# A planned HGRN2 + ReGLU kernel: new waits for the first loads and weight slices, one score mask on ScalarE and GpSimd, and even FFN groups

## The chip, the core and the metric

The kernel runs on one core of a Trainium2 chip. The metric is the device time of one execution in microseconds (us). TensorE is called PE here, VectorE DVE, ScalarE ACT, GpSimd POOL and SyncE SP, as the profile has them.

## What is computed

A gated linear attention is followed by a gated feed-forward layer. For 4 batches and 8 heads of 48 columns, 768 tokens each:

```python
f = 1.0 / (1.0 + np.exp(-f_logit))
for t in range(S):
    state = f[:, :, t, :, None] * state + einsum('bhd,bhe->bhde', k[:, :, t], v[:, :, t])
    y[:, :, t] = einsum('bhd,bhde->bhe', q[:, :, t], state)
x = y.transpose(0, 2, 1, 3).reshape(3072, 384)
out = (np.maximum(x @ w_gate, 0) * (x @ w_val)) @ w_out      # 384 -> 1536 -> 384
```

Inputs and output are float32; the kernel works in bfloat16 on PE.

## The kernel before

**Tiling.** The attention is done in chunks. Six *units* take 256 tokens of one batch each (`attention_unit(d, b)`; units 0 to 3 are d = 0 with b = 0 to 3, units 4 and 5 are d = 1 with b = 0, 1). The rest is done in chunks of 128 tokens (`attention_front` and `attention`). For a unit, f, k, q and v are loaded (one DMA of 384 KB each, named f0, k0, ... by unit). ACT takes the log of the gate (exp, then ln: L615, L617). PE sums it along the tokens (L626, L627), and ACT exponentiates the sums (L639, L642). POOL scales k (L644) and DVE scales q (L647) into `hats`. PE transposes these (L678), and DVE and ACT copy them to SBUF (L686, L687). PE makes the scores (L722) in four PSUM banks. DVE multiplies each bank with a causal mask (`seen`, L727) into `ptm`. POOL spreads v into `vpad` (L653). PE makes the states (L699), the products of masked scores and v (`intra`, L757, in two halves for units 0 and 1), and the product with the state (`inter`, L740). The result is copied to `xT` (L781 on ACT, L782 on DVE), the input of the FFN.

**FFN.** `ffn_hidden` makes a gate and a value product of three matmuls each (L959) for one of 12 columns j of 128. ACT takes the relu (L965), and DVE multiplies both (L970) into `gT`. `ffn_out` (L996) multiplies with w_out. A pair of units gives 512 tokens. `groups` says which j are done for each half of the tokens alone (256 columns) and which for all (512 columns). For the first pair `lead = 3` puts three gates ahead of their values.

**Weights.** w_gate and w_val come in three slices each (wg0, wv0 hold j = 0 to 2; wg1, wv1 hold 3 to 5; wg2, wv2 hold 6 to 11) and w_out in three (wo0 to wo2). POOL issues these DMAs (L534), and they convert to bfloat16. SP issues all other DMAs: loads of units (L500) and of chunks (L512), transposes by DMA from unit 4 on (L577, L583), and stores (L1016).

**Order.** The program is made once, ahead of the run. Every operation is recorded with its engine, reads, writes and an assumed duration. `Plan` then lists the operations of each engine in the order in which a model of the chip would start them. `Rings` is its model of DMA. Each engine runs its list in order, and an instruction waits on semaphores for what it reads. So an assumed duration changes only the order; no work depends on it. The list `first` orders the first loads and weight slices by hand: `f2` is a load that waits for nothing and `f3@wg1` is one whose issue waits until the slice wg1 has landed. Since SP and POOL are in order, all that stands behind such a wait is held too. Loads that follow wait for an earlier one, so that `flight` = 3 (units) or 4 (chunks) are under way. Gaps that the model leaves on PE before 24 us are filled with idle matmuls (L1077), which keep PE busy and yield nothing.

```python
first = "f0 k0 wg0@k0 q0 f1 v0 wv0@v0 wg1 wv1@k0+wg0 wg2@f0+wv0 wv2@wg1 q1 k1 wo1@k1+wv1 v1 f2
         wo0@f2+wg2 wo2@f1+wv2 f3@wg1 q2@wg0 k2 v2@wv2 q3@wg0 v3@wg0 k3"
groups = {0: [(0, 2, range(0, 6)), (2, 4, range(0, 6)), (0, 4, range(6, NJ))],
          1: [(0, 2, range(0, 4)), (2, 4, range(0, 4)), (0, 4, range(4, NJ))],
          2: [(0, 2, range(0, 3)), (2, 4, range(0, 3)), (0, 4, range(3, NJ))]}
```

Of the kernel before, what the change touches and what calls it, by code (L numbers as in the profile page):

```python
# [45 lines left out]
class Rings:  # L46
# [19 lines left out]

    def through(self, t, work, n, mine=None):

        for a, b, left in self.other[n]:
            if b <= t:  # L70
                continue
            if t < a:
                if work <= a - t:
                    return t + work
                work -= a - t
                t = a
            left = left if mine is None else mine
            if work <= (b - t) * left:
                return t + work / left
            work -= (b - t) * left  # L80
            t = b
        return t + work

    def room(self):
        over = self.pushed - self.AHEAD
# [12 lines left out]

    def hw(self, op, at, took):
        begin = max(at + (took - 0.05 if op.ring == "turn" else op.lat), self.hw_free)  # L100
        if op.descs == 1024 and self.log:
            self.skew = 0.65 * min(1.0, max(0.0, 1.0 - (self.hw_free - at - took) / 1.2))
        else:
            self.skew = 0.0
        self.hw_free = self.through(begin, op.flow, 1)
        self.made[0].append((begin, self.hw_free, 1.0))
        self.log.append((begin, self.hw_free, self.pushed, op.descs))
        self.pushed += op.descs
        late = 0.0 if at < 5.0 or op.descs < 500 else self.LATE[2 if op.ring == "turn" else at > self.EARLY]
        return self.hw_free + late + (0.8 if op.ring == "turn" else self.LAND + self.skew)  # L110

    def sw(self, at, flow):
        work, left, tail, rest, lag = flow
        begin = max(at, self.sw_free)
        main = self.through(begin, work, 0, 1.0 - left)
        self.sw_free = main + tail
        self.made[1].append((begin, main, left))
        self.made[1].append((main, self.sw_free, rest))
        return self.sw_free + self.LAND + lag


class Plan:
# [209 lines left out]
def bass_hgrn2_outer__then__ffn_reglu_kernel(  # L332
# [95 lines left out]

    def fill(eng, name, ap, value, cols, prio, key=None):
        e = engine[eng]  # L430
        add(eng, lambda: e.memset(ap, value), [], [key or name], occ=0.06 + cols / 1000.0, prio=prio)

    def triangle(t, name, base, prio, step=-1):
        fill("POOL", name, t[:], 1.0, 128, prio)
        add("POOL", lambda: gp.affine_select(out=t[:], in_=t[:], compare_op=ALU.is_ge, fill=0.0, base=base,
                                             pattern=[[1, 128]], channel_multiplier=step),
            [name], [name], occ=0.3, prio=prio)

    for t, name, base in ((upto, "upto", 0), (below, "below", -1)):
        triangle(t, name, base, -20)  # L440
# [1 line left out]
    fill("POOL", "ident", ident[:], 0.0, 128, -16)  # L442
    add("POOL", lambda: gp.affine_select(out=ident[:], in_=ident[:], compare_op=ALU.not_equal, fill=1.0,
                                         base=0, pattern=[[-1, 128]], channel_multiplier=1),
        ["ident"], ["ident"], occ=0.3, prio=-16)
    for i in range(2):
        for t, name, base in ((seen[i], f"seen{i}", -i), (later[i], f"later{i}", 64 - i)):
            fill("POOL", name, t[:], 1.0, 128, -15)
            add("POOL", lambda t=t, base=base, i=i: gp.affine_select(out=t[:], in_=t[:], compare_op=ALU.is_ge, fill=0.0, base=base,
                                                                     pattern=[[i, 2], [1, 64]], channel_multiplier=-1),  # L450
                [name], [name], occ=0.3, prio=-15)
# [41 lines left out]
    def load_unit(n, d, b, after=()):  # L493
        t = ld[n]
        row = NL[n] * 2 * HD
        c, pr = 2 * d + b // 2, b % 2
        src = bass.AP(tensor=srcs[n].tensor, offset=b * H * S * D + 2 * d * C * D, ap=[[2 * D, 128], [S * D, H], [1, 2 * D]])
        dst = bass.AP(tensor=t, offset=slot_of(n, c, pr) * 2 * HD, ap=[[row, 128], [2 * D, H], [1, 2 * D]])
        last = tails.get("load")
        op = add("SP", lambda: sy.dma_start(dst, src), [], in_keys(n, c, 2 * pr, 2 * pr + 2), occ=0.5, lat=1.13,  # L500
                 prio=d * 200 + b * 10, after=after, follows=[last] if last else [])
        tails["load"] = op
        dma(op, f"{n}{slot_of(n, c, pr)}" , 1.79 if n == "f" and d + b == 0 else 1.24 if d == 0 else 1.45, 1, 1024)
        return op

    def load(n, c, b0, b1, after=()):
# [18 lines left out]
    def load_w(nm, s, after):  # L525
        j0, j1 = WB[nm][s:s + 2]
        if nm == "wo":
            src = bass.AP(tensor=w_out.tensor, offset=j0 * 128 * DM, ap=[[DM, 128], [128 * DM, j1 - j0], [1, DM]])
            dst = wo[:, j0:j1, :]
        else:  # L530
            src = bass.AP(tensor=wsrc[nm].tensor, offset=j0 * 128, ap=[[DFF, 128], [128 * DFF, NK], [1, (j1 - j0) * 128]])
            dst = (wg if nm == "wg" else wv)[:, :, j0 * 128:j1 * 128]
        last = tails.get("load_w")
        op = add("POOL", lambda: gp.dma_start(dst, src), [], [f"{nm}{s}"], occ=0.8, lat=2.05, prio=0 if nm != "wo" and s < 1 else 20, after=after,  # L534
                 follows=[last] if last else [])
        tails["load_w"] = op
        dma(op, f"{nm}{s}", (2.0, 0.22, 0.7, 0.5, 0.0) if nm == "wo" else (1.47, 0.25, 0.7, 0.85, 0.9 if s < 1 else 0.2) if j1 - j0 < 6 else (2.9, 0.14, 0.3, 0.3, 0.0), ring="sw")
        return op

    loads, done = [], {}  # L540
# [59 lines left out]
    def attention_unit(d, b):  # L600
# [113 lines left out]
        for i in range(2):  # L714
# [9 lines left out]
                return mm  # L724
            chain("scores", "PE", scores, [k_ for k_ in both if k_[-2] == "0" or k_.startswith(f"qkT{q0 + i}_")], sj, occ=0.215, lat=PE_L, prio=P + 5, opens=sj, tile="64x64")
            for j in range(2):
                add("DVE", lambda i=i, j=j, s=sj[j]: ve.tensor_tensor(  # L727
                    ptm_all[:, m0 + i, j, :, :], s.ap[:, :].rearrange("p (n t) -> p n t", n=NP),
                    seen[i][:].rearrange("p i t -> p (i t)").unsqueeze(1).to_broadcast([128, NP, C]), ALU.mult),
                    [sj[j], f"seen{i}"], [f"ptm{m0 + i}_{j}"], prio=P + 6, **dve_t(512))  # L730
                pk.append(f"ptm{m0 + i}_{j}")
        if d:
            states()
# [210 lines left out]

    hidden = [0]

    def ffn_hidden(c, b0, b1, j, queue=None):
# [8 lines left out]
        def proj(bank, wt):  # L956
# [10 lines left out]
        def values():  # L967
            chain("ffn", "PE", proj(val, wv), xk + [w_key("wv", j)], [val], occ=pe_t(n, n, n), lat=PE_L,
                  prio=P + 1000, opens=[val])
            add("DVE", lambda: ve.tensor_tensor(gT[gi][:, j, n0:n1], relu[ri][:, 0:n], val.ap[:, 0:n], ALU.mult),  # L970
                [val, f"relu{ri}"], [f"gT{gi}_{j}_{b}" for b in range(b0, b1)], prio=P, **dve_t(n))

        if queue is None:
            values()
        else:
            queue.append(values)

    OJ = 4
    held = {}
# [6 lines left out]
    def ffn_out(g, bs, cuts=(0, DM)):  # L986
# [16 lines left out]
        for b, z in [(b, z) for b in bs for z in parts]:  # L1003
# [16 lines left out]
            if z == (0, DM):  # L1020
                tails[f"osb{oi}"] = op

    groups = {0: [(0, 2, range(0, 6)), (2, 4, range(0, 6)), (0, 4, range(6, NJ))],
              1: [(0, 2, range(0, 4)), (2, 4, range(0, 4)), (0, 4, range(4, NJ))],
              2: [(0, 2, range(0, 3)), (2, 4, range(0, 3)), (0, 4, range(3, NJ))]}
    pend = []
    for c in range(NC):
        if c in units:
# [15 lines left out]
                    attention(c, b + e)  # L1044
        for b0, b1, js in groups.get(c, [(0, 4, range(NJ))]):
            len0, js = len(pend), list(js)
            lead = 3 if c == 0 and b1 == 2 else 0
            queue = []
            for j in js[:lead]:
                ffn_hidden(c, b0, b1, j, queue)  # L1050
            for values in queue:
                values()
# [25 lines left out]

    fillers, at, begun = {}, pl.free0["PE"], False
    for op in order["PE"]:  # L1080
        gap, (n, each, rest) = op.start - at, (66, 0.055, 0.25) if at < 5.0 else (128, 0.107, 0.3)
# [82 lines left out]
```

## Time and profile before

| what | value |
|---|---|
| median of 3 runs | 193.06 us (192.57 to 194.32) |
| the profiled execution, its own time | 193.54 us |
| its span (first to last instruction) | 191.8 us |
| PE busy | 184.1 us (96%) |
| DVE, ACT, POOL busy | 106.6, 107.9, 71.7 us |
| read from HBM | 25.95 MB |
| first useful matmul, first FFN matmul | 5.72 us, 15.61 us |
| first FFN matmul of 512 columns (slice wg2) | 30.70 us |

PE's busy time includes the idle matmuls and the time in which its clock is halved, so the 96% are not all useful work. The row of slices in the profile shows the granted clock as PEclk in tenths. A chain of waits is read from its end: each piece was released by the one ahead of it.

### The profile page before, as it was taken

What the parts mean: (1) busy time and instruction counts of PE and PEld (TensorE: products, weight loads), DVE (VectorE), ACT (ScalarE), POOL (GpSimd) and SP (SyncE); (2) the same over time, 40 slices, a digit from 0 to 9 for tenths busy, and PEclk for the clock granted to TensorE, in tenths of its full rate; (3) what the DMA queues carried; (4) which work ended last, traced back from release to release, by engine and by line L of the source; (5) the groups of instructions that cost most, each with busy time, mean ns of one, the idle gap of its engine ahead of it and who ended that gap; (6) DMA issues with size and microseconds to landing.
All of it is one profiled execution on the core that took longest, in us unless ns stands there. A gap on an engine that the chain in (4) does not pass through costs nothing.

```text
span 191.8 us, 5282 instructions
## 1 busy us (share of the span) xinstructions
PE 184.1 (96%) x2209; PEld 111.3 (58%) x2209; DVE 106.6 (56%) x202; ACT 107.9 (56%) x236; POOL 71.7 (37%) x112
## 2 busy tenths in 40 slices
PE   8878699999999999999999999999999999999995
PEld 8747476466686556766445565654555555554554
DVE  5277744739996879453477284643624723443300
ACT  3865478625399765655937739548442543334322
POOL 8667521066375193863552735700900000000000
PEclk9999979999999999999999999999999999999999
DMA  5999999989998999999989989777852120011113
GB/s 152 318 251 219 218 244 205 230 234 285 235 254 157 175 225 171 233 237 231 214 173 194 196 171 223 166 156 172 178 121 71 44 82 8 33 41 44 41 48 116
DMA packets 102343, 32.45 MB, mean 169 GB/s; under 512 B 95408, under 2 KB 102320, under 8 KB 102320
## 3 DMA queue, kind: packets, MB, share of 16 engines
q1 hardware_dynamic: 98336, 28.58, 68.2%
q0 software_dynamic: 3984, 3.54, 11.4%
q8 instruction: 17, 0.28, 0.6%
q14 instruction: 6, 0.05, 0.1%
HBM read 25.95 MB, written 4.72 MB: 160 GB/s over the span
## 4 chain that ended last, share of the span: by engine, by line
PE 85%; DMA 7%; SPq 4%; DVE 3%; POOL 0%; issue 0%; ACT 0%
PE ps L959 49%; PE ps L996 23%; DMA v_in<-in_v_dram 7%; SPq L500 4%; PE ps L757 2%; PE ps L872 2%; DVE ptm L727 1%; PE ps L805 1%; PE ps L902 1%; PE ps L740 1%; PE ps L699 1%; DVE hats L647 1%; PE ps L722 1%; PE ps L912 1%; PE ps L935 1%; PE ps L908 1%
## 5 line engine op out<-in xcount | busy, mean ns | idle before, releaser
L970 DVE TENSOR_TENSOR gT<-relu,ps 128x512 bf16<-128x512 bf16 (+1 forms) x85 | 50.8, 603 | 55.2 <-PE ps L959 39.3
L959 PE MATMUL ps<-xT,wg 128*128 128x512 bf16 (+1 forms) x255 | 61.1, 350 | 0.5 <-ACT xT L781 0.5
L959 PE MATMUL ps<-xT,wv 128*128 128x512 bf16 (+1 forms) x255 | 60.9, 348 | 0.0
L965 ACT ACTIVATE relu<-ps 128x512 bf16<-128x512 f32 (+1 forms) x85 | 44.8, 533 | 28.3 <-PE ps L959 28.2
L996 PE MATMUL ps<-wo,gT 128*128 128x384 bf16 (+2 forms) x312 | 52.0, 314 | 0.0
L996 PEld LDWEIGHTS ps<-wo,gT 128*128 128x128 bf16 x312 | 28.2, 98 | 18.1
L959 PEld LDWEIGHTS ps<-xT,wg 128*128 128x128 bf16 x255 | 24.3, 99 | 20.4 <-ACT xT L781 0.7
L959 PEld LDWEIGHTS ps<-xT,wv 128*128 128x128 bf16 x255 | 24.0, 98 | 19.7
L1011 ACT ACTIVATE osb<-ps 128x384 f32<-128x384 f32 (+2 forms) x25 | 11.7, 474 | 30.6 <-PE ps L996 30.5
L827 POOL TENSOR_TENSOR hats<-k_in,expo 128x384 bf16<-128x384 f32 x12 | 11.8, 996 | 23.2 <-ACT expo L815 12.1
L879 DVE TENSOR_TENSOR ptm<-ps,tri 128x512 bf16<-128x512 f32 x24 | 15.2, 684 | 4.1 <-PE ps L872 4.1
L644 POOL TENSOR_TENSOR hats<-k_in,expo 128x384 bf16<-128x384 f32 x12 | 12.6, 1064 | 11.0 <-DMA k_in<-in_k_dram 8.1
L727 DVE TENSOR_TENSOR ptm<-ps,seen 128x512 bf16<-128x512 f32 x24 | 14.9, 681 | 1.3 <-PE ps L722 1.2
L830 POOL TENSOR_TENSOR hats<-q_in,expo 128x384 bf16<-128x384 f32 x12 | 11.8, 998 | 0.3 <-DMA q_in<-in_q_dram 0.3
L597 POOL TENSOR_TENSOR st<-ssum,dec 128x384 bf16<-128x384 f32 x8 | 6.5, 828 | 11.8 <-DVE ssum L595 11.8
L595 DVE TENSOR_TENSOR ssum<-ps,st 128x384 f32<-128x384 f32 x16 | 8.5, 550 | 3.0 <-PE ps L935 2.7
L597 POOL TENSOR_TENSOR st<-ssum,decu 128x384 bf16<-128x384 f32 x8 | 6.6, 828 | 8.3 <-DVE ssum L595 7.8
L781 ACT ACTIVATE xT<-ps 128x384 bf16<-128x384 f32 x8 | 4.7, 601 | 6.2 <-PE ps L757 6.2
L615 ACT ACTIVATE f_in<-f_in 128x768 f32<-128x768 f32 (+1 forms) x7 | 5.1, 748 | 5.3 <-DMA f_in<-in_f_logit_dram 5.3
L653 POOL CAST vpad<-v_in 128x384 bf16<-128x384 f32 x12 | 6.1, 531 | 3.4 <-DMA v_in<-in_v_dram 3.4
L815 ACT ACTIVATE expo<-ps 128x384 f32<-128x384 f32 x12 | 5.9, 492 | 1.7 <-PE ps L808 1.4
L925 ACT ACTIVATE xn<-ps 128x384 bf16<-128x384 f32 x8 | 3.9, 488 | 5.2 <-PE ps L912 5.2
(91 smaller groups left out, 174.7 us busy)
## 6 DMA issues: line engine op xcount, KB each, us to landing
f_in<-in_f_logit_dram SPq DMA_DIRECT2D x12, 384.0 KB, 5.7
k_in<-in_k_dram SPq DMA_DIRECT2D x12, 384.0 KB, 4.9
q_in<-in_q_dram SPq DMA_DIRECT2D x12, 384.0 KB, 5.3
v_in<-in_v_dram SPq DMA_DIRECT2D x12, 384.0 KB, 5.2
out_dram<-osb SPq DMA_DIRECT2D x23, 192.0 KB, 2.2
wo<-in_moe_w_out_dram POOLq DMA_DIRECT2D x3, 384.0 KB, 11.0
wg<-in_moe_w_gate_dram POOLq DMA_DIRECT2D x2, 288.0 KB, 7.5
wv<-in_moe_w_val_dram POOLq DMA_DIRECT2D x2, 288.0 KB, 7.4
```

What stands on the lines that cost most here:

```text
L595: add("DVE", lambda: ve.tensor_tensor(tmp[:, :], kv.ap[:, 0:HD], s_old[:, :], ALU.add), [kv, f"S{b}_{(c + 1) % 2}"], [key], prio=P + 8, ** ...
L597: add("POOL", lambda: gp.tensor_tensor(t4(s_new), t4(tmp), rate, ALU.mult), [key] + dk, [f"S{b}_{c % 2}"], prio=P + 8, occ=0.79, lat=0.23)
L644: add("POOL", lambda i=i, hi=hi, ei=ei: gp.tensor_tensor(hats[:, hi, 1, :, 0:D], by_i["k"][:, i, :, :], expo[:, ei, 1, :].rearrange("p (h ...
L727: add("DVE", lambda i=i, j=j, s=sj[j]: ve.tensor_tensor(ptm_all[:, m0 + i, j, :, :], s.ap[:, :].rearrange("p (n t) -> p n t", n=NP), seen[ ...
L827: add("POOL", lambda: gp.tensor_tensor(hk, kin[:, b % 2, :, :], ex[:, 1, :].rearrange("p (h d) -> p h d", h=H), ALU.mult), in_keys("k", c, ...
L830: add("POOL", lambda: gp.tensor_tensor(hq, qin[:, b % 2, :, :], ex[:, 0, :].rearrange("p (h d) -> p h d", h=H), ALU.mult), in_keys("q", c, ...
L879: add("DVE", lambda j=j, s=s: ve.tensor_tensor(ptm[mi][:, j, :, :], s.ap[:, :].rearrange("p (n t) -> p n t", n=NP), mask, ALU.mult), [s, " ...
L959: mm = te.matmul(bank.ap[:, 0:n], wt[:, kt, j * 128:(j + 1) * 128], xT[xi][:, b0:b1, kt, :], start=(kt == 0), stop=(kt == NK - 1))
L965: add("ACT", lambda: sc.activation(relu[ri][:, 0:n], gate.ap[:, 0:n], AF.Relu), [gate], [f"relu{ri}"], prio=P, **act_t(n))
L970: add("DVE", lambda: ve.tensor_tensor(gT[gi][:, j, n0:n1], relu[ri][:, 0:n], val.ap[:, 0:n], ALU.mult), [val, f"relu{ri}"], [f"gT{gi}_{j}_ ...
L996: mm = te.matmul(o[b, z].ap[:, 0:z[1] - z[0]], gT[gi][:, j, b * C:(b + 1) * C], wo[:, j, z[0]:z[1]], start=(j == 0), stop=(j == NJ - 1))
L1011: add("ACT", lambda to=to, of=of: sc.activation(to, of(), AF.Copy), [o[b, z]], [f"osb{oi}_{z[0]}"], prio=P, **act_t(z[1] - z[0]))
```

## The change

The masks: of unit 0's four score banks, the last (i = 1, j = 1) is no longer masked by DVE out of PSUM. ACT copies it to `ptm`, and POOL multiplies it there with the mask, in place, in bfloat16.

The first loads: `first` has other waits. On SP, f2 now waits for wg1, and f3, q2, k2, v2 and v3 follow without waits that could still hold them; q3 waits for wv2, and v3 goes ahead of q3. On POOL, wv1 still waits for wg0. Ahead of unit 1's k on POOL stand now the mask of unit 0 and one state product. The issues of wg2 and wv2 stand ahead of unit 1's `vpad`, and wo0 waits for wv1 and f2.

The FFN: each group of halves takes j = 0 to 5 in all three pairs (18 groups each instead of 18, 16 and 15), and `lead` is gone: each value follows its gate.

The model: durations of fills, selects and first loads, the flows of weight slices, the landing times, and pauses at fixed times (`FETCH`, `HOLD`) in which no DMA moves. They change the order alone. In the order that comes out, PE starts unit 0's `intra` in two halves with 9 idle matmuls between them, takes gate and value of j = 0 ahead of unit 1's transposes, and does j = 1 to 5 in between the steps of unit 1, whose states now follow both halves of `intra`. SP issues the four DMA transposes of units 4 and 5 together and the next chunk's k, q and v behind them.

```diff
-    EARLY, LATE = 14.0, (1.0, 0.8, 1.0)
-    AHEAD, LAND = 1500, 0.65
+    EARLY, LATE = 14.0, (0.4, 0.8, 0.8)
+    AHEAD, LAND, FRONT = 1500, 0.52, 42.0
+    FETCH, HOLD = (9.4, 17.8, 25.8, 33.3, 46.5, 51.0, 56.0), 0.94
...
+    by_pool = {(0, 0, 1, 1)}
     flight = (3, 4)
-    first = "f0 k0 wg0@k0 q0 f1 v0 wv0@v0 wg1 wv1@k0+wg0 wg2@f0+wv0 wv2@wg1 q1 k1 wo1@k1+wv1 v1 f2 wo0@f2+wg2 wo2@f1+wv2 f3@wg1 q2@wg0 k2 v2@wv2 q3@wg0 v3@wg0 k3".split()
+    first = "f0 k0 wg0@k0 q0 f1 v0 wv0@v0 wg1@k0 wv1@wg0 wg2@f0+wv0 q1 wv2@q1+wg1 k1 v1 f2@wg1 wo0@f2+wv1 wo1@wg2 wo2@f2+wv2 f3 q2 k2@wg1 v2 v3 q3@wv2 k3@wg0".split()
...
-        op = add("SP", ... occ=0.5, lat=1.13,
+        op = add("SP", ... occ=0.5, lat=1.35 if n == "f" and d + b == 0 else 1.55 if d == 0 else 1.13,
...
             for j in range(2):
-                add("DVE", lambda i=i, j=j, s=sj[j]: ve.tensor_tensor(
-                    ptm_all[:, m0 + i, j, :, :], s.ap[:, :].rearrange("p (n t) -> p n t", n=NP),
-                    seen[i][:]...to_broadcast([128, NP, C]), ALU.mult),
-                    [sj[j], f"seen{i}"], [f"ptm{m0 + i}_{j}"], prio=P + 6, **dve_t(512))
+                to, key_m = ptm_all[:, m0 + i, j, :, :], f"ptm{m0 + i}_{j}"
...
+                if (d, b, i, j) in by_pool:
+                    add("ACT", lambda to=to, of=of: sc.activation(to, of(), AF.Copy), [sj[j]], [key_m + "raw"], prio=P + 4, **act_t(512))
+                    add("POOL", lambda to=to, mask=mask: gp.tensor_tensor(to, to, mask, ALU.mult), [key_m + "raw", f"seen{i}"],
+                        [key_m], prio=P + 1, occ=1.15, lat=0.23)
+                else:
+                    add("DVE", lambda to=to, of=of, mask=mask: ve.tensor_tensor(to, of(), mask, ALU.mult),
+                        [sj[j], f"seen{i}"], [key_m, key_m + "raw"], prio=P + 6, **dve_t(512))
...
-              1: [(0, 2, range(0, 4)), (2, 4, range(0, 4)), (0, 4, range(4, NJ))],
-              2: [(0, 2, range(0, 3)), (2, 4, range(0, 3)), (0, 4, range(3, NJ))]}
+              1: [(0, 2, range(0, 6)), (2, 4, range(0, 6)), (0, 4, range(6, NJ))],
+              2: [(0, 2, range(0, 6)), (2, 4, range(0, 6)), (0, 4, range(6, NJ))]}
...
-            lead = 3 if c == 0 and b1 == 2 else 0
...
             for at, j in enumerate(js):
-                if at >= lead:
-                    ffn_hidden(c, b0, b1, j)
+                ffn_hidden(c, b0, b1, j)
```

More of the change, by code (lines that the diff above doesn't have):

```diff
@@ L67, in through @@
     def through(self, t, work, n, mine=None):
[L69 to L82, printed above, removed]
+        while True:
+            rate, until = 1.0, 1e9
+            for a in self.FETCH:
+                if a <= t < a + self.HOLD:
+                    t = a + self.HOLD
+                elif t < a:
+                    until = min(until, a)
+            for a, b, left in self.other[n]:
+                if a <= t < b:
+                    rate, until = left if mine is None else mine, min(until, b)
+                elif t < a:
+                    until = min(until, a)
+            if work <= (until - t) * rate:
+                return t + work / rate
+            work -= (until - t) * rate
+            t = until
     def room(self):
@@ L100, in hw @@
         begin = max(at + (took - 0.05 if op.ring == "turn" else op.lat), self.hw_free)
-        if op.descs == 1024 and self.log:
+        if op.descs == 1024 and at > self.FRONT:
             self.skew = 0.65 * min(1.0, max(0.0, 1.0 - (self.hw_free - at - took) / 1.2))
@@ L112, in sw @@
     def sw(self, at, flow):
-        work, left, tail, rest, lag = flow
+        work, left, cost = flow
         begin = max(at, self.sw_free)
[L115 to L119, printed above, removed]
+        self.sw_free = self.through(begin, work, 0, 1.0 - cost)
+        self.made[1].append((begin, self.sw_free, left))
+        return self.sw_free + self.LAND
 class Plan:
@@ L430, in fill @@
         e = engine[eng]
-        add(eng, lambda: e.memset(ap, value), [], [key or name], occ=0.06 + cols / 1000.0, prio=prio)
+        add(eng, lambda: e.memset(ap, value), [], [key or name],
+            occ=0.03 + cols * 0.00087 if eng == "POOL" else 0.05 + cols * 0.0004, prio=prio)
     def triangle(t, name, base, prio, step=-1):
@@ L444, in bass_hgrn2_outer__then__ffn_reglu_kernel @@
                                          base=0, pattern=[[-1, 128]], channel_multiplier=1),
-        ["ident"], ["ident"], occ=0.3, prio=-16)
+        ["ident"], ["ident"], occ=0.245, prio=-16)
     for i in range(2):
@@ L499, in load_unit @@
         last = tails.get("load")
-        op = add("SP", lambda: sy.dma_start(dst, src), [], in_keys(n, c, 2 * pr, 2 * pr + 2), occ=0.5, lat=1.13,
+        op = add("SP", lambda: sy.dma_start(dst, src), [], in_keys(n, c, 2 * pr, 2 * pr + 2), occ=0.5, lat=1.35 if n == "f" and d + b == 0 else 1.55 if d == 0 else 1.13,
                  prio=d * 200 + b * 10, after=after, follows=[last] if last else [])
         tails["load"] = op
-        dma(op, f"{n}{slot_of(n, c, pr)}" , 1.79 if n == "f" and d + b == 0 else 1.24 if d == 0 else 1.45, 1, 1024)
+        dma(op, f"{n}{slot_of(n, c, pr)}" , 1.62 if n == "f" and d + b == 0 else 1.12 if d == 0 else 1.45, 1, 1024)
         return op
@@ L533, in load_w @@
         last = tails.get("load_w")
-        op = add("POOL", lambda: gp.dma_start(dst, src), [], [f"{nm}{s}"], occ=0.8, lat=2.05, prio=0 if nm != "wo" and s < 1 else 20, after=after,
+        op = add("POOL", lambda: gp.dma_start(dst, src), [], [f"{nm}{s}"], occ=0.8, lat=2.95, prio=0 if nm != "wo" and s < 1 else 20, after=after,
                  follows=[last] if last else [])
         tails["load_w"] = op
-        dma(op, f"{nm}{s}", (2.0, 0.22, 0.7, 0.5, 0.0) if nm == "wo" else (1.47, 0.25, 0.7, 0.85, 0.9 if s < 1 else 0.2) if j1 - j0 < 6 else (2.9, 0.14, 0.3, 0.3, 0.0), ring="sw")
+        dma(op, f"{nm}{s}", (2.2, 0.21, 0.21) if nm == "wo" else (1.52, 0.25, 0.32) if j1 - j0 < 6 else (2.39, 0.12, 0.14), ring="sw")
         return op
@@ L945, in bass_hgrn2_outer__then__ffn_reglu_kernel, with ffn_hidden @@
     hidden = [0]
-    def ffn_hidden(c, b0, b1, j, queue=None):
+    def ffn_hidden(c, b0, b1, j):
         xi, gi, ri = c % NX, c % NG, hidden[0] % NR
@@ L966, in ffn_hidden @@
             prio=P, **act_t(n))
[L967 to L976, printed above, removed]
+        chain("ffn", "PE", proj(val, wv), xk + [w_key("wv", j)], [val], occ=pe_t(n, n, n), lat=PE_L,
+              prio=P + 1000, opens=[val])
+        add("DVE", lambda: ve.tensor_tensor(gT[gi][:, j, n0:n1], relu[ri][:, 0:n], val.ap[:, 0:n], ALU.mult),
+            [val, f"relu{ri}"], [f"gT{gi}_{j}_{b}" for b in range(b0, b1)], prio=P, **dve_t(n))
     OJ = 4
@@ L1080, in bass_hgrn2_outer__then__ffn_reglu_kernel @@
     for op in order["PE"]:
-        gap, (n, each, rest) = op.start - at, (66, 0.055, 0.25) if at < 5.0 else (128, 0.107, 0.3)
+        gap, (n, each, rest) = op.start - at, (70, 0.059, 0.25) if at < 5.0 else (128, 0.107, 0.3)
         if begun and op.start <= warm_until:
```

12 lines of the change are left out of this document (4 added, 8 removed).

## The prediction

> **What bounds the kernel now.** The page comes first, for shares and clock.
>
> ```profile
> PE   8878699999999999999999999999999999999995
> ...
> PEclk9999979999999999999999999999999999999999
> ```
>
> After the fifth slice (24 us) PE is full. The list of PE's own waits agrees: its eight waits over 0.15 us sum to 5 us, and all lie before 22 us. The longest:
>
> ```profile
> PE ps L699 <- POOL vpad L653: 1.8, 1, 1.8
> ```
>
> The chain of waits says where it comes from (start, us, what): v of unit 1 lands 12.5 us after its issue, POOL spreads it, and PE makes the states.
>
> ```profile
> 7.87 12.50 DMA v_in<-in_v_dram
> 20.37 0.06 issue
> 20.43 0.96 POOL vpad L653 x2
> 21.39 0.14 issue
> 21.52 0.61 PE ps L699 x16
> ```
>
> This gap has a second price. Here are stretches of 3.4 us, with the busy time of PE first and the granted clock third from the end:
>
> ```profile
> 12.80:16.20 3.40, 2.53 (x104) 1.71 (x103) 2.98 (x6) 1.11 (x3) 2.28 (x3) 1.00 1.25 234
> ...
> 19.60:23.00 3.40, 1.61 (x85) 1.24 (x83) 2.18 (x6) 1.30 (x3) 2.45 (x4) 1.00 1.18 206
> 23.00:26.40 3.40, 3.40 (x33) 2.10 (x31) 1.61 (x5) 2.27 (x5) 1.59 (x2) 0.51 1.16 278
> 26.40:29.80 3.40, 3.40 (x38) 3.06 (x36) 2.21 (x6) 3.24 (x10) 0.04 (x1) 0.99 1.18 205
> ```
>
> A stretch with PE busy for 1.61 of 3.40 us is followed by one at half clock; one with 2.53 is not. Half clock costs 1.7 us of work. Last, the orders on PE, POOL and ACT around the change:
>
> ```profile
> 13.98 0.42 PE L757 MATMUL ps<-ptm,vpad 64*32 64x128 bf16 x32 [0.18 <-DVE ptm L727]
> ...
> 15.61 0.50 PE L959 MATMUL ps<-xT,wg 128*128 128x256 bf16 x3 [0.48 <-ACT xT L781]
> ```
>
> ```profile
> 13.53 0.77 POOL L534 DMA_DIRECT2D wv<-in_moe_w_val_dram  x1 [1.58 <-DMA wg<-in_moe_w_gate_dram]
> 14.69 1.94 POOL L644 TENSOR_TENSOR hats<-k_in,expo 128x384 bf16<-128x384 f32 x2 [0.39 <-DMA k_in<-in_k_dram]
> 16.60 0.82 POOL L597 TENSOR_TENSOR st<-ssum,decu 128x384 bf16<-128x384 f32 x1
> 17.37 0.80 POOL L534 DMA_DIRECT2D wg<-in_moe_w_gate_dram  x1
> 20.43 0.95 POOL L653 CAST vpad<-v_in 128x384 bf16<-128x384 f32 x2 [2.26 <-DMA v_in<-in_v_dram]
> 21.33 0.78 POOL L534 DMA_DIRECT2D wv<-in_moe_w_val_dram  x1
> ```
>
> ```profile
> 22.08 0.84 ACT L615 ACTIVATE f_in<-f_in 128x768 f32<-128x768 f32 x1 [1.93 <-DMA f_in<-in_f_logit_dram]
> ```
>
> One mark measures the change: the first gate of 512 columns, at 30.70 us. The same work lies ahead of it in both kernels. From there to the end (161.1 us) PE never waits, so the end moves with the mark.
>
> **The mask, and what it waits for.** DVE is spared one mask of 0.62 us (2.48 for four, L727). ACT gets a copy of 512 columns (0.60, as L687), hidden in its idle 1.86 us ahead of 14.50. POOL's multiply is not in this trace. Below: a CAST takes 505 ns for 384 columns, so 0.67 for 512. Above: the product with two f32 inputs (L644) takes 996, so 1.33. The product of L597 (828) gives 1.10, and I take that, as a plain product from SBUF. But its place matters more. On POOL it stands behind the issue of wv1, which waits for wg0: that issue ran from 13.53 to 14.30. The mask therefore ends at 14.30 + 1.10 = 15.4, and the second half of unit 0's product starts at 15.5 instead of 13.98. From there to the first FFN matmul took 1.63, so the FFN starts at 17.1 instead of 15.6: **1.5 us later**. By the bounds of the mask this is 1.1 to 1.75.
>
> **Where the wait for v goes.** In the new order PE has pairs j = 0 to 4 and both halves of the product to do before it needs the states of unit 1. POOL does mask, state product (0.82) and unit 1's k (1.94) until 18.1, issues wg2 and wv2 until 19.7, and spreads v at its landing, 20.4, as before. v is needed from 21.3 on, so its 1.79 us are covered. If v is later than 21, PE loses it one for one, as before.
>
> **The walk to the mark.** From 17.1: the work up to the mark is 24 gates and values of 256 columns (0.327 each: 7.85), 16 transposes 0.89, 32 scores 0.57, 16 states 0.45, 64 products 0.67, 12 inter 0.28, and the sums of unit 2 (0.50): 11.2, and some 0.3 for changes of shape. Without any wait the mark is at 28.6. Two waits remain. Unit 1's scores end at 20.2, and its four masks take DVE until 22.7. Then PE does half a product, states and pair 5 until 24.1, while DVE does three products (1.1), one `xT` (0.5) and the state (0.5) until 24.7: 0.65 of wait ahead of `inter`. Then `inter`, sums (25.55) and the second `xT` on ACT: 0.25. The twelve gates and values of units 0 and 1's second half end at 25.8 + 3.95 = **29.75**. wv2 is needed 0.65 later; it landed at 30.2 and is now issued 2.4 us sooner. If that cover fails, at most 0.7 is lost.
>
> **The clock.** In the stretch 12.8 to 16.2 PE would now be busy with one half product (0.4), 9 idle matmuls (0.55) and the second half with `inter` (0.65): 1.6 of 3.4, as in the stretch that brought the half clock before. So 16.2 to 19.6 would run at half clock. PE has work there from 17.1 on: 2.5 us, of which 1.25 are lost. Mark: **31.0**. The half clock of 23.0 to 26.4 goes, since its gap is gone.
>
> The Trainium skill, "TensorE: Matmul & The Clock Gate", section "HAM oscillation — how this bites in real kernels", says that the clock falls after an idle gap of more than about 3.4 us. By that rule neither kernel's gap would halve it, and the mark would stand at 29.75. The trace differs: a gap of 1.79 us was followed by 3.4 us at 0.51.
>
> **f of unit 2.** Its load was issued at 10.24 and landed at 22.05; now SP holds it until wg1 lands, 18.8. The fastest f load took 3.5 us from issue, the median 5.7, the slowest 11.8. Between 14.7 and 22.1 two loads (v1, f2) took 3.7 each; between 22.1 and 38.7 three (f3, q2, k2) took 5.5 each, beside wg2 and wv2. So f2 lands between 22.3 and 26.1; I take 23.5, the near end, since wg2's issue now ends at 18.9 and leaves the DMA engines to f2 for a while. ACT needs 1.75 for exp and ln, so the sums can start at 25.3: in time for the walk at half clock (26.3), hardly for the other. Behind f2 on ACT stand relu 5 and `xT`; behind it on POOL wo0, needed at 39. Each us beyond 24.4 is one on PE.
>
> **Edits that cost nothing.** Even groups: 10 more pairs of 256-column triples, 0.654 against 0.648: 0.06. Five more relus and products (0.4) fall on ACT and DVE, which idle 45% there. The four DMA transposes together hold k, q and v of the next chunk until 65; with 1.2 to 1.8 each for six loads and 4.7 for two transposes the scores are possible at 80 and due at 83. Without that cover 1 to 2 us would be lost. Unit 3's k landed at 43.8; its transposes are due at 46.5.
>
> **Sum.** Mark 31.0 against 30.70, 0.06 for the groups, and something for f2: +0.4. The profiled execution took 193.54 (1.73 around the span), so 193.95; it lies 0.48 above the median, so **193.5**. This case's own range is 192.4 to 195.2. Within 1% (191.1 to 195.0) is about what a measurement of this kernel can't tell from no change.
>
> **Rivals.**
> *B: the late start costs no clock.* PE is then at the mark between 28.6 (no wait) and 29.75: 2.1 to 0.95 less, 191.0 to 192.1; a wg0 landing 0.5 sooner (7.7 us against 7.2 for wv0) takes off as much again. For it: one half clock alone was seen, and with borders laid elsewhere the stretch around the gap is denser. Against it: 1.6 and 1.61 of 3.4 are alike.
> *C: f2 comes late, and the kernel is slower.* At 5.5 us per load f2 lands at 26.1. The sums start at 27.9, the gates at 28.7, the mark is at 32.7: +2.0. PE then idles 2 us before the sums, which by the rows above brings another half clock: up to +3.7. Time 195.0 to 196.8. It decides from a landing of 24.4 on. For it: f2 enters the queue just when wg2 begins, and the slowest q load (15.0 us) and k load (17.7) were under way in that company. Against it: little else is in its own queue.
> *D: only the wait moves:* v late beyond 21.3, mark as before, 193.1.
>
> **How the numbers follow.** Forecast 0.36 (0.06 of it over +1%), B 0.26 (0.17 beyond -1%), C 0.34, all slower, D 0.04. So faster 0.17, same 0.43, slower 0.40. The range leaves out one in ten at each end, half of B's fast part and the top of C: 190.7 to 196.2.
>
> **What would show it.** POOL's mask starting at 14.3, right after wv1's issue; the first FFN matmul near 17.1; clock 0.5 in 16.2 to 19.6 and full in 23.0 to 26.4; the exp of f2 on ACT at 23.5; no wait on `vpad`; the mark at 31.0 and from there 161 us. It is wrong if the first FFN matmul comes before 16.5, if f2 lands after 24.4, or if PE waits anywhere behind the mark.

## The result, and the profile after

The changed kernel is slower: 201.09 us median (200.47 to 202.32) against 193.14 (192.57 to 194.32) for the kernel before on the same chip, a ratio of 1.041 (95% interval 1.037 to 1.046). The profiled execution took 200.51 us with a span of 198.8. Comparisons leave out executions more than 1.5% above the fastest of the same kernel.

On the page (40 slices of 5.0 us), PE has one hole and the clock one dip, both between 24 and 36 us:

```profile
PE   8678807999999999999999999999999999999995
...
PEclk9999985999999999999999999999999999999999
```

The list of PE's waits has a single large entry where the kernel before had the wait for `vpad`. PE waits for ACT's log of the gate; the longest of these waits is 6.2 us, and `vpad` no longer appears:

```profile
PE ps L627 <- ACT bneg L618: 7.4, 3, 6.2
```

The chain of waits, followed back from 40 us (start, us, what), says why. wg1 lands at 18.6, and only then is f2 issued. f2 needs 10.41 us, then ACT makes exp and ln, and PE makes the sums of unit 2:

```profile
11.04 7.58 DMA wg<-in_moe_w_gate_dram
18.61 0.02 issue
18.63 10.41 DMA f_in<-in_f_logit_dram
29.05 0.02 issue
29.07 0.85 ACT f_in L616
29.92 0.02 issue
29.94 0.85 ACT bneg L618
30.80 0.05 issue
30.84 0.50 PE ps L627
```

The order on POOL shows what f2 met. The mask starts right behind wv1's issue. wg2 is issued at 17.90 and wv2 at 18.90, on both sides of f2's issue at 18.63:

```profile
13.04 0.78 POOL L535 DMA_DIRECT2D wv<-in_moe_w_val_dram  x1 [1.22 <-DMA wg<-in_moe_w_gate_dram]
13.84 1.17 POOL L733 TENSOR_TENSOR ptm<-ptm,seen 128x512 bf16<-128x512 bf16 x1
...
17.90 0.80 POOL L535 DMA_DIRECT2D wg<-in_moe_w_gate_dram  x1
18.90 0.78 POOL L535 DMA_DIRECT2D wv<-in_moe_w_val_dram  x1 [0.20 <-issue]
```

On PE, the second half product and the first FFN matmul come 0.4 us sooner than forecast; then follow the hole and, at 37.08 instead of 30.70, the mark (the first gate of 512 columns):

```profile
15.05 0.42 PE L764 MATMUL ps<-ptm,vpad 64*32 64x128 bf16 x32 [0.71 <-POOL ptm L733]
...
16.68 0.50 PE L966 MATMUL ps<-xT,wg 128*128 128x256 bf16 x3 [0.53 <-ACT xT L788]
...
30.84 0.50 PE L627 MATMUL ps<-bneg,upto 128*128 128x384 bf16 x1 [6.24 <-ACT bneg L618]
...
37.08 0.81 PE L966 MATMUL ps<-xT,wg 128*128 128x512 bf16 x3
```

Stretches of 3.4 us, PE's busy time first and the granted clock third from the end: the stretch that was to be at half clock (16.20) is at full clock, and the clock falls only in the hole and behind it:

```profile
12.80:16.20 3.40, 2.44 (x98) 1.71 (x98) 2.34 (x5) 1.31 (x5) 2.92 (x4) 1.00 1.27 233
16.20:19.60 3.40, 2.92 (x51) 2.56 (x55) 1.77 (x4) 1.97 (x5) 3.20 (x4) 1.00 0.96 144
...
26.40:29.80 3.40, 0.00 (x0) 0.00 (x0) 0.00 (x0) 0.73 (x1) 0.46 (x1) 0.72 1.15 284
29.80:33.20 3.40, 2.36 (x18) 1.58 (x19) 0.98 (x2) 3.19 (x9) 3.14 (x5) 0.50 1.03 217
33.20:36.60 3.40, 3.40 (x26) 2.77 (x25) 1.42 (x4) 2.19 (x7) 1.50 (x2) 0.78 1.20 203
```

From the mark to the end it takes 161.7 us (161.1 before). The mark is 6.4 us later and the span 7.0 us longer, so 0.6 us of the loss lies behind the mark.

### The profile page after: what moved, and what is told of

It reads as the page before. It is cut to its first block, busy times and chain, and to the rows that moved or that the text cites. A ratio compares the mean times of both kernels' runs of the same rounds, so it can differ in the third digit from the quotient of the medians.

```text
span 198.8 us, 5363 instructions
## 1 busy us (share of the span) xinstructions
PE 185.0 (93%) x2238; PEld 113.5 (57%) x2238; DVE 106.3 (53%) x204; ACT 111.1 (56%) x244; POOL 72.2 (36%) x113
## 4 chain that ended last, share of the span: by engine, by line
PE 72%; DMA 14%; SPq 5%; POOL 4%; DVE 2%; ACT 1%; issue 1%
PE ps L966 42%; PE ps L997 21%; DMA f_in<-in_f_logit_dram 5%; DMA wg<-in_moe_w_gate_dram 4%; DMA v_in<-in_v_dram 2%; DMA out_dram<-osb 2%; SPq L578 2%; SPq L501 2%; PE ps L879 1%; POOL st L598 1%; DVE ptm L736 1%; SPq L1017 1%; PE ps L679 1%; PE ps L812 1%; POOL hats L837 1%
## 5 line engine op out<-in xcount | busy, mean ns | idle before, releaser
L976 DVE TENSOR_TENSOR gT<-relu,ps 128x512 bf16<-128x512 bf16 (+1 forms) x90 | 51.5, 579 | 64.8 <-PE ps L966 34.9
L966 PE MATMUL ps<-xT,wg 128*128 128x512 bf16 (+1 forms) x270 | 62.4, 341 | 0.5 <-ACT xT L788 0.5
L972 ACT ACTIVATE relu<-ps 128x512 bf16<-128x512 f32 (+1 forms) x90 | 45.9, 514 | 29.9 <-PE ps L966 29.5
L966 PE MATMUL ps<-xT,wv 128*128 128x512 bf16 (+1 forms) x270 | 62.2, 340 | 0.0
L966 PEld LDWEIGHTS ps<-xT,wg 128*128 128x128 bf16 x270 | 25.7, 99 | 19.2 <-ACT xT L788 0.7
L966 PEld LDWEIGHTS ps<-xT,wv 128*128 128x128 bf16 x270 | 25.7, 99 | 18.9
L1012 ACT ACTIVATE osb<-ps 128x384 f32<-128x384 f32 (+2 forms) x25 | 11.9, 475 | 33.8 <-PE ps L997 30.4
L736 DVE TENSOR_TENSOR ptm<-ps,seen 128x512 bf16<-128x512 f32 x23 | 14.4, 682 | 1.4 <-PE ps L723 1.4
L627 PE MATMUL ps<-bneg,upto 128*128 128x384 bf16 (+1 forms) x10 | 3.0, 316 | 7.4 <-ACT bneg L618 7.4
```

The lines of the kernel that those rows point to most:

```text
L736: add("DVE", lambda to=to, of=of, mask=mask: ve.tensor_tensor(to, of(), mask, ALU.mult), [sj[j], f"seen{i}"], [key_m, key_m + "raw"], prio ...
L966: mm = te.matmul(bank.ap[:, 0:n], wt[:, kt, j * 128:(j + 1) * 128], xT[xi][:, b0:b1, kt, :], start=(kt == 0), stop=(kt == NK - 1))
L1012: add("ACT", lambda to=to, of=of: sc.activation(to, of(), AF.Copy), [o[b, z]], [f"osb{oi}_{z[0]}"], prio=P, **act_t(z[1] - z[0]))
```

## The experiments

In the code excerpts, `...` stands for code that is not shown, a name like `sums_of_unit_2` for a lookup in the lists, and a line that begins with # is a remark.

**f2 alone (e1, e2).** In e1 f2 waits for nothing and f3, the next load on SP, takes over the wait; every list of instructions stays. e2 adds the same wait to f2 in the kernel before.

```diff
# e1, on the kernel after (all orders fixed, then the waits are made)
+    done["f2"].deps.pop(done["wg1"]); done["f3"].deps[done["wg1"]] = "raw"
# e2, on the kernel before
+    done["f2"].deps[done["wg1"]] = "raw"
+    done["f2"].start = done["f3"].start - 0.1
```

> The kernel after, with every engine's order as it is, but f2 no longer waits for wg1 (f3, right behind it on SP, takes over that wait, so that only f2 moves). Theory 1, the whole loss is f2's hold: f2 is issued by 11, lands before 22, PE's wait of 6.2 us ahead of unit 2's sums is gone, and no half clock follows at 28 to 35. The first FFN matmul stays at 16.7; with 11.5 us of walk from there and 0.7 to 2.3 of small waits the first gate of 512 columns comes at 29 to 30.5, and 161.5 from there give a time of 192.0 to 193.8, within 1% of before. Theory 2, other parts of the new order (the mask on POOL, the gates without lead, the wait of wv1) cost most of the 8 us: the mark stays behind 33 and the time above 195.5.

> The kernel before, every order as it is, with one wait added: f2 is issued when wg1 has landed (about 18.8). Theory 1: f2 then lands 8 to 11 us later, 27 to 30, its exp on ACT holds the relus behind it, PE waits 4 to 6 us ahead of unit 2's sums and runs some us at half clock behind that; the mark moves from 30.7 to 35.5 to 37.5, and the time is 198 to 200.5. Theory 2: the hold alone costs little in the old order (f2 lands by 24.5 as a quick load of 3.5 to 5.7 us would, mark by 31.7), and the time stays below 195.

e1 took 193.94 us, 1.006 of the kernel before (1.003 to 1.009): theory 1 holds, 0.1 us above its range. In its profile PE starts the sums of unit 2 without a wait, and the mark is where theory 1 had it:

```profile
24.62 0.34 PE L627 MATMUL ps<-bneg,upto 128*128 128x384 bf16 x1
...
29.84 0.81 PE L966 MATMUL ps<-xT,wg 128*128 128x512 bf16 x3
```

So f2's wait is 3.5% of the time, 6.8 us, and everything else in the change together 0.6%. e2 took 195.20 us, 1.014 (1.009 to 1.019): slower, but by 2.7 us and not by 5 to 8. That is nearly its theory 2: f2 landed at 24.7, 6.04 us after its issue, and the mark is at 31.60.

```profile
18.67 6.04 DMA f_in<-in_f_logit_dram
```

The same wait costs less than half in the old order. In that order only wg2 is issued ahead of this point; wv2 follows at 21.2, 2.5 us into f2's flight.

**What f2 met (e3, e11).** Both are the kernel after with f2's wait as it is. e3 moves wg2 and wv2 behind unit 1's `vpad` and holds them until f2 has landed. e11 moves wv2 alone behind `vpad`, its place before.

```diff
# e3
# order["POOL"]: wg2, wv2 moved to just ahead of wo0
+    done["wg2"].deps[done["f2"]] = "raw"; done["wv2"].deps[done["f2"]] = "raw"
# e11
# order["POOL"]: wv2 moved to just behind unit 1's vpad
```

> The kernel after with f2 still waiting for wg1 (issue at 18.6), but the issues of wg2 and wv2 moved behind unit 1's vpad on POOL and made to wait until f2 has landed. Theory A, f2 took 10.4 us because the two large slices were streaming: it now lands in 3.5 to 5.7 us, at 22 to 24.5, and PE waits less than 1 us for it. wg2, issued at 23 to 25, then comes late: it took 7 to 10 us from issue, so the mark is at 31 to 34 and the time at 193 to 196. Theory B, a load issued at that moment is slow anyway (other loads and slices ahead of it): f2 lands at 27 to 29 as before, wg2 another 8 us behind it, the mark is at 36 or later and the time at 199 or more.

> The kernel after with f2 waiting for wg1 as it does, and one issue moved on POOL: wv2 behind unit 1's vpad, as in the kernel before, so issued at 21 instead of 18.9. Theory A, f2 is delayed by each large slice that stands ahead of it (3.4 us with none, 10.4 with both): with wg2 alone it takes 5.5 to 7, lands at 24.2 to 25.7, PE waits 1.3 to 3 us for the sums instead of 6.2, mark at 31 to 33, time 195 to 197.5. Theory B, wg2 alone delays it as much: lands at 28 to 29, time 200 or more.

f2's time from issue to landing, first e3, then e11:

```profile
18.64 3.37 DMA f_in<-in_f_logit_dram
```

```profile
19.03 6.01 DMA f_in<-in_f_logit_dram
```

With neither large slice issued 3.37 us, with wg2 ahead and wv2 some 2.5 us behind 6.04 and 6.01 (two orders, e2 and e11), with both within 1 us of f2 10.41. So theory A holds for f2's flight. Two more runs with both slices, e4 and e8 below, agree: ACT's exp of f2 starts 9.7 and 9.5 us after f2's issue. In e11 PE waits 2.36 us ahead of the sums, the mark is at 32.61, and the time is 196.80 (1.018, 1.012 to 1.024), all as theory A had it. e3's time missed its range: 198.65 (1.031, 1.026 to 1.036). wv2, now issued at 23.1, took 10.64 us, and PE waited 2.40 us for it. (The granted clock of the profiled execution was 0.85 throughout, so only the transfers and this wait are read from it; the rest of e3's 5.9 us was not followed.) Letting f2 go first and the slices after it moves a part of the loss to the slices.

**The place of f2's work (e5).** f2 stays late, but the planner is told that it cannot be used before 29 us. So ACT's exp and ln and PE's sums move behind the twelve gates and values.

```diff
+    for op in pl.ops:
+        if op.eng == "ACT" and "f2_0" in op.reads and "f2_0" in op.writes: op.floor = 29.0
     order = pl.schedule(...)
```

> The kernel after with f2 still waiting for wg1, but the planner is told that f2 cannot be used before 29 us. DMA issues and waits of the first 30 us stay; ACT's exp and ln of f2 and PE's sums of unit 2 come behind the twelve gates and values of 256 columns and three gates or values of 512, instead of ahead of them. Theory 1a, the loss is the place of f2's work in the in-order lists of ACT and PE, not f2's lateness: f2 still lands at 28 to 29.5, PE no longer waits for it, the mark comes at 29.3 to 30.5, time 193 to 194.5. Theory 1b, unit 2 itself is late and the wait moves on: PE waits 3 us or more somewhere before 60, time above 197.

Theory 1a holds up to the mark. The exp of f2 starts at 29.05 as in the kernel after, PE does not wait for it, and the mark is at 29.55:

```profile
29.05 0.84 ACT L616 ACTIVATE f_in<-f_in 128x768 f32<-128x768 f32 x1
```

```profile
29.55 0.81 PE L966 MATMUL ps<-xT,wg 128*128 128x512 bf16 x3
```

But the time is 196.26 (1.014, 1.006 to 1.021), between the two theories, because from the mark to the end it takes 164.8 us; PE idles 2.2 us between 42 and 114 us, 1.1 of it without a releaser. So the hole at 24.6 is a matter of order: in-order lists put f2's exp ahead of a relu, an `xT` and PE's next work. Told when f2 really lands, the planner gets back 2.7% of the time, 5 us. The later order then loses 3 us behind the mark; why it does was not followed further.

**The clock in the hole (e4, e8).** Idle matmuls on PE ahead of the sums: 92 of 128 columns (e4), 24 of 512 (e8).

```diff
+    fillers[sums_of_unit_2] = [warm(128)] * 92     # e8: [warm(512)] * 24
```

> The kernel after with nothing changed but 92 idle matmuls of 128 columns (0.061 us each in the trace of before, 5.6 together) on PE ahead of unit 2's sums, where PE waited 6.2 us. f2 lands at 29 as it did. If the half clock from 28 to 35 comes of that gap, it goes: sums at 30.9, twelve gates and values at full clock, mark at 35.2 to 35.7 instead of 37.1, time 199.2 to 199.8. If the clock falls there for another reason, the mark stays at 37 and the time at 201.

> The kernel after with 24 idle matmuls of 512 columns (about 0.22 us each, 5.2 together) on PE ahead of unit 2's sums, in place of the 92 narrow ones that PE interrupted for 2.0 us. If the half clock comes of an idle PE, all stretches up to the mark run at full clock, the mark is at 35.2 to 35.8 and the time 199.2 to 199.8, with a mean clock of 1.00. If the half clock is there without idle time, the time stays at 201.

e4 gave 200.82 (1.041, 1.035 to 1.046) and is inconclusive: PE paused 2.03 us among the idle matmuls with no releaser, and the clock fell to 0.61 behind that. e8 gave 199.16 (1.030, 1.023 to 1.036), 1.1% less than the kernel after; its executions with a mean clock of 1.00 took 197.6 to 199.3. In its profile the clock is 1.00 from 26.4 to 33.2, where the kernel after had 0.72 and 0.50. So the half clock behind the hole is worth some 2 us and PE's waiting itself the other 5. The rows of the kernel after give the same estimate: half of 2.36 us and 0.22 of 3.40 us are 1.9.

**The early idle matmuls (e10).** e1 without the 9 idle matmuls between unit 0's half products and the 5 ahead of the first FFN matmul.

```diff
+    for op in list(fillers):
+        if op.start > 13.5: del fillers[op]
```

> The kernel after with f2 waiting for no slice, and without the 14 idle matmuls (9 and 5, 1.2 us together) that stood between unit 0's two half products and ahead of the first FFN matmul. PE is then busy for 1.3 instead of 2.4 us of 12.8 to 16.2. The prediction's reading, that so thin a stretch halves the clock of the next: 16.2 to 19.6 at 0.5 in most executions, mean clock 0.991, mark 0.9 to 1.3 us later than 29.84, time 194.8 to 195.6. Rival: the clock there does not depend on the idle matmuls, time as with f2 free, 193.9.

194.99 (1.011, 1.007 to 1.016), and all six executions had a mean clock of 0.991 or less, where e1 had 1.000 in seven of ten. The clock falls in and behind the thin stretch:

```profile
12.80:16.20 3.40, 1.42 (x80) 0.99 (x84) 2.44 (x5) 0.70 (x3) 2.46 (x3) 0.74 1.26 237
16.20:19.60 3.40, 2.23 (x22) 1.25 (x15) 0.42 (x1) 1.43 (x3) 1.75 (x3) 0.50 1.23 233
```

**The mask and the groups (e6, e7).** Both have f2 free. e6 puts the fourth mask back on DVE, e7 takes the groups of before.

```diff
# both: f2 free and f3 behind wg1, as in e1
# e6
+    by_pool = set()
# e7
+    1: [(0, 2, range(0, 4)), (2, 4, range(0, 4)), (0, 4, range(4, NJ))],
+    2: [(0, 2, range(0, 3)), (2, 4, range(0, 3)), (0, 4, range(3, NJ))]}
```

> The kernel after with f2 waiting for no slice (f3 holds that wait) and all four masks on DVE. With f2 free and the mask on POOL the time was 193.94 and the first FFN matmul came at 16.76, with PE waiting 0.79 for POOL's mask. Theory M, the late mask is the rest of the loss: the first FFN matmul comes at 15.5 to 15.9, the mark 0.8 to 1.1 sooner, at 28.8 to 29.1, time 192.9 to 193.2. Theory W, the slice wv1, which landed at 21.1, hides it: PE waits 1.0 to 1.6 ahead of the value of j = 3 instead, the mark stays at 29.5 to 29.9 and the time at 193.6 to 194.

> The kernel after with f2 waiting for no slice (f3 holds that wait) and the groups of before (4 and 3 columns j of half width in the second and third pair). The first 40 us are ordered as with the new groups, so the mark stays at 29.8. From the mark to the end took 161.1 in the kernel before and 161.56 with f2 free. If the new groups are that difference: 161.1, time 193.4 to 193.6. If they cost only the 0.06 of the prediction: time 193.8 to 194.

Neither mends anything. e6 took 195.42 (1.012, 1.006 to 1.017): its first FFN matmul came at 16.16, 0.6 sooner than in e1, but PE was busy for only 2.10 us of 12.8 to 16.2, the next stretch ran at 0.52, and all six executions were at 0.991 or less:

```profile
12.80:16.20 3.40, 2.10 (x93) 1.36 (x94) 3.07 (x7) 1.42 (x4) 2.30 (x3) 1.00 1.26 248
16.20:19.60 3.40, 3.40 (x25) 2.94 (x26) 1.11 (x2) 1.34 (x3) 1.77 (x4) 0.52 1.24 214
```

So e6 doesn't decide between its theories. e7 took 194.76 (1.008, 1.004 to 1.013), above both expectations; from the mark to the end took 161.9 us, against 161.56 in e1. The new groups cost nothing that can be measured.

**The kernel before, and instructions (e14, e9, e12, e13, e15, e16, e17).** e14 is the kernel before again. e9 puts 8 idle matmuls of 512 columns into its wait for v. The rest take instructions away at the start: 18 idle matmuls of 512 columns instead of 82 of 66 (e12; e13 the like on e1; e15 with e9's 8), then 13 (e16; e17 with 6 in the wait).

```diff
# e9, e15: * 8; e17: * 6
+    fillers[states_of_unit_1] = [warm(512)] * 8
# e12, e13, e15: 0.25; e16, e17: 0.345
-    ... (66, 0.055, 0.25) if at < 5.0
+    ... (512, 0.25, 0.25) if at < 5.0
```

> The kernel before once more, unchanged, for a profile. In an execution at a mean clock of 1.000 the half clock of 23.0 to 26.4 is not there. If its removal were worth the 1.7 us of the prediction, the mark is at 29.0; if PE then waits for instructions as in the kernels that reached this place early, a gap without a releaser ends at 27.4 to 27.7 and the mark is at 29.6 to 29.9, which fits the 192.65 of the undisturbed runs.

> The kernel before with 8 idle matmuls of 512 columns (0.22 us each, 1.7 together) on PE ahead of unit 1's states, where PE waited 1.8 us for v. Nothing else moves. If that gap is what halves the clock in 23.0 to 26.4 us in some executions (mean clock 0.991) and not in others (1.000), all executions now run at 1.000, the mark comes at 29.0 instead of 30.7, and the median falls by what the half clock costs (1.7 us) times its frequency, to 192.0 to 192.9. If the half clock has another cause, some executions still show 0.991 and the median stays at 193.

> The kernel before with its 82 idle matmuls of 66 columns at the start replaced by 18 of 512 columns (4.3 us instead of 4.7), so that PE runs 64 instructions fewer ahead of the first useful matmul. Theory I: what PE cannot pass before 27.4 to 27.7 is the arrival of its next block of instructions (one packet of 16 KB on the instruction queue at 25.0 in every kernel; gaps that nothing releases end at 27.45, 27.59, 27.40 and 27.73 in four kernels). With 64 fewer instructions ahead the block ends later in the work, PE does not wait for it ahead of the mark, and undisturbed executions have the mark at 28.9 to 29.2 and take 191.7 to 192.2 instead of 192.65. Rival: the code does not matter for the kernel before, its undisturbed executions stay at 192.5 to 192.8.

> The kernel after with f2 waiting for no slice and 17 idle matmuls of 512 columns in place of the 75 of 70 at the start. Theory I: the gap of 0.35 us at 27.45 goes, the mark comes at 29.3 to 29.5 instead of 29.84, time 193.4 to 193.6 instead of 193.94; still slower than before, so what is left of the new order costs 1 us by itself (first FFN matmul at 16.7). Rival: the gap moves to another place and the time stays at 193.9.

> The kernel before with 18 wide idle matmuls at the start and 8 of 512 columns in PE's wait for v, the edits of two runs together. With the gap filled alone the kernel took 194.0 at full clock, since PE waited 1.68 us at 27.40 without a releaser. Theory I: with 64 instructions fewer that gap goes, the mark is at 28.9 to 29.2 in nearly all executions, and the median 191.8 to 192.3 is below the kernel before. Rival: the idle matmuls in the gap cost time by themselves, 193.5 to 194.

> The kernel before with 13 idle matmuls of 512 columns at its start instead of 82 of 66. The 18 of the earlier run took 0.33 us each and not 0.25, which put the first useful matmul 1.0 us late; 13 take 4.3, so it comes at 5.7 as before. Theory I: PE runs 69 instructions fewer ahead of the work, the gap of 0.6 us without a releaser at 27.0 goes, the mark is at 28.7 to 29.0 instead of 29.41 and the time 192.0 to 192.3 instead of 192.7. Rival: the gaps without a releaser come at other places (0.5 and 0.6 ahead of the mark, 1.1 behind it, in the run with 18), and the time is 192.7 to 194.5.

> The same start, and 6 idle matmuls of 512 columns (1.4 us) in PE's wait for v. If both steps hold (no gap for want of instructions, no half clock behind the wait), the mark is at 28.7 to 29.0 in all executions and the median 191.8 to 192.2, below the kernel before. Rival as above: the time is 193 or more, and spread.

e14, at a mean clock of 1.000, took 192.67. Its wait for v is only 1.00, and a gap without a releaser ends at 26.99:

```profile
20.56 0.59 PE L699 MATMUL ps<-vpad,hats 64*128 64x96 bf16 x16 [1.00 <-POOL vpad L653]
...
26.99 0.28 PE L959 MATMUL ps<-xT,wg 128*128 128x256 bf16 x1 [0.61 <-issue]
...
29.41 0.81 PE L959 MATMUL ps<-xT,wg 128*128 128x512 bf16 x3
```

So without the half clock the mark is at 29.41, between the two expectations, and from there to the end it takes 161.5. But the states started 0.96 us sooner here too, so not all of the 1.29 us at the mark is the clock's. In e9 the later gap grew to 1.68 us, and the time to 194.02 (1.006, 1.002 to 1.009): filling a wait with idle matmuls only moved it. 3 of e9's 12 executions still had a mean clock of 0.991 (6 of 17 of the kernel before in this comparison). So filling this wait did not remove the half clock from all of them; where it lay in those three no record shows.

```profile
27.40 0.50 PE L959 MATMUL ps<-xT,wg 128*128 128x256 bf16 x3 [1.68 <-issue]
```

The wide matmuls took 0.33 to 0.37 us each at the start and not 0.25, so e12, e13 and e15 began 1 to 1.7 us late: 194.56, 194.01 and 196.06 (192.9 to 199.1), with ratios of 1.006 to 1.007, but by its median e15 is 1.6% slower. e16 and e17 began within 0.5 us of plan: 196.10 (1.015, 1.012 to 1.019) and 195.58 (1.013, 1.009 to 1.016). e16 is slower than both its expectations, and e17 fits its rival. In e16 the gap at 27 was gone and the mark at 29.10, 0.1 later than theory I had it. But new gaps without a releaser came, 0.50 and 0.61 ahead of the mark, 1.6 and 0.8 behind it. The rival is right that they move. No version beat the kernel before.

## Why the prediction was wrong

**The step that failed is f2's landing.** The prediction saw the mechanism, and rival C describes it in place and sequence. The size was wrong. In the sum f2 has a term of some 0.04 us (0.4 less 0.30 for the mark and 0.06 for the groups); in the run PE waited 6.24 us for it. The landing was mis-sized twice. The near end, 23.5, was taken because "wg2's issue now ends at 18.9 and leaves the DMA engines to f2 for a while"; but the same order issues wv2 at 18.9, 2.4 us sooner than before, which the prediction counted only as a cover for wv2's own use. e11 shows that the place of this one issue is worth 4.4 us of f2's flight. And the far end, 26.1, goes by a mean time per load (5.5; from the issue at 18.8 that would be 24.3, and no other start is given), though the slowest f load in the same paragraph took 11.8: a bound on one transfer was taken from a rate of three. By 11.8 f2 lands at 30.4, and C's upper end moves from 196.8 to 201.1, about what was measured. That it comes so close is partly luck: the load of 11.8 was f2 itself in the old order, where it landed at 22.05 behind v1, which landed at 20.37. f2 took 10.41; the exp came at 29.07, not 23.5. From there C's own steps are right: 1.77 us later the sums start, 30.84, and the half clock comes. "Behind f2 on ACT stand relu 5 and `xT`" was right too, and e5 shows that the place in the list is what makes the lateness cost.

**The half clock in 16.2 to 19.6 did not come**, because the sum for 12.8 to 16.2 left work out. It had 1.6 us; PE was busy for 2.44. Missing were the 5 idle matmuls ahead of the first FFN matmul (0.46) and unit 1's totals (0.35), both of them in order ahead of 16.2. With the idle matmuls taken away (e10, 1.42 busy) the half clock came. So the addition was wrong. But the reading of the stretches is no rule either. Half clock (0.52 and 0.51) followed 2.10 us of busy time in e6 and 2.25 in e17. In e2's profile full clock followed 1.61 and 1.43:

```profile
19.60:23.00 3.40, 1.61 (x83) 1.24 (x83) 2.15 (x6) 0.38 (x1) 2.45 (x4) 1.00 1.08 190
23.00:26.40 3.40, 1.43 (x22) 0.89 (x21) 1.06 (x3) 1.66 (x3) 1.63 (x2) 1.00 1.18 285
26.40:29.80 3.40, 3.22 (x36) 2.61 (x34) 1.98 (x5) 3.37 (x12) 0.00 (x0) 1.00 1.19 205
```

The other three executions of e2 had a mean of 0.991. What decides between the two stays open. Of 87 executions of the kernel before in these comparisons, 21 had a mean clock of 0.991, the rest 0.999 or more. One stretch of 3.4 us at half clock takes 0.009 off the mean clock of 192 us (an estimate). So the half clock that the prediction removed seems to come in about one execution of four, and the profile had caught one; where it lay in the executions without a profile is not shown.

The Trainium skill, "TensorE: Matmul & The Clock Gate", section "HAM oscillation — how this bites in real kernels", puts the limit at an idle gap of about 3.4 us. The hole of 6.24 us agrees with it (clock 0.50 behind it). e10 does not: its longest gap was 1.77 us, and every execution lost clock. Nor does e6: between 10 us and the fall of its clock at 16.2 us its longest gap was 0.54 us.

**What held.** The mask started behind wv1's issue, at 13.84 (14.3 forecast, wg0 having landed 0.5 sooner), and took 1.17 (1.10). The second half product came at 15.05 (15.5) and the first FFN matmul at 16.68 (17.1). The wait for v was covered. From the mark to the end took 161.7 (161). With f2 free the walk holds: e1's mark is at 29.84, and 29.75 was forecast without a half clock. That e1's 193.94 lies near the forecast of 193.5 is luck: 193.5 holds 1.25 us of half clock that did not come, and without it rival B had 192.1 at most, 1.8 us less than e1 took.

**What stays open.** The 0.6% that e1 is slower than the kernel before. Its profiled execution, the fastest of ten, has its mark 0.43 us later than e14 and the same time behind it, 161.56 against 161.49. The other 0.7 us were not found.

## What to carry to other kernels

When a load is made to wait, list every transfer that will be issued within some us of its new place, those moved ahead of it by the same change included, and bound its flight by the slowest comparable transfer of the trace, or by the landing of the transfers at its side, and not by a mean. Then ask what stands behind its first reader on the in-order engines: a late load that is read late costs nothing at its place, one that is read first stops everything. And before a fault of one profiled execution is counted as a gain, see in the other executions how often it is there.

## What the runs showed of the hardware

- A load of 384 KB on SP's queue took 3.37 us with neither of the two weight slices of 576 KB issued, 6.0 with one ahead of it and the other some 2.5 us behind, and 10.4 with both within 1 us. It landed shortly behind the last of them: wg2 landed at 23.7 and 24.0 in e2 and e11 and f2 at 24.7 and 25.0, wv2 at 28.5 in the kernel after and f2 at 29.0. The Trainium skill, "DMA: Bandwidth & Descriptors", section "Queues, rings and completion order", says that each DMA engine takes turns between its queues, packet by packet. That a load beside the slices takes several times as long agrees with it; no run here shows the turns themselves.
- PE gaps of about 1.8 us were followed by half clock in some executions (1.79 us in the kernel before, for 3.4 us; 1.77 in e10) and not in another (1.81 and 1.97 in e2's profile). In the kernel before, the 21 executions at 0.991 have a median of 193.97 us and the other 66 one of 192.68. How much of these 1.3 us is the clock itself is not shown, since the longer wait that goes with it costs time too (1.79 us before, 1.00 in e14).
- PE stops without any releaser until 27.0 to 27.7 us in the orders that get there early (0.35 us in e1, 0.61 in e14, 1.68 in e9, 2.03 in e4). The profile shows one packet of 16 KB on an instruction queue between 24 and 26 us in each of them. Fewer idle matmuls at the start moved both the packets and the gaps (e16). That PE waits for its instructions there fits, but no record shows it.
